# A fused attention and soft mixture-of-experts kernel: blocks 0 and 1 taken in turn by quarters of w_in's columns, raw words and results in one 64 KB tile

## The chip, the core and the metric

The kernel runs on one core of one Trainium2 chip. The metric is the device time of one execution in microseconds (us), lower is better. Engines are named as in the profile: PE is TensorE (matrix products), DVE is VectorE, ACT is ScalarE, POOL is GpSimd, and SP is the queue that issues the DMAs.

## The reference, cut to what matters

Three layers follow one another. The middle one gets its weights `w_in` (512 x 2048) and `w_out` (2048 x 512) as float64 words, which the kernel turns into float32 itself.

```
a  = softmax(x @ state.T / 8);  xread = a @ state
a2 = softmax(state @ x.T / 8);  sread = a2 @ x
y  = concat(xread, sread)                  # 8 batches x 544 rows x 512
h  = y @ w_in;  g = h * sigmoid(h);  z = g @ w_out
logits = z @ phi                           # 32 slots
d = softmax(logits over rows);  c = softmax(logits over slots)
slots = d.T @ z;  out = c @ (relu(slots @ w1[e]) @ w2[e])
```

## The kernel before, in words

**Blocks and steps.** The 8 batches are blocks 0 to 7 of 512 rows each; a ninth, shorter block (number 8) holds the rows of `sread`. For a block k, `a_scores` multiplies its tokens `xT` with the state (PE, tiles `sc`), `a_split`, `a_soft1`, `a_soft2` and `a_soft3` make the softmax on ACT and DVE (tiles `e`, `s`, `asm`, `tm`) and leave it as `ar` in two parts, a rounded one (ACT) and the remainder (DVE for blocks 0 and 1, POOL later). `a_eT` and `a_sread` make `sread` (tiles `eT`, `sr`, `srT`; they need the tokens `xk`). `wb` multiplies the state with a quarter of `w_in`'s columns (tiles `wbp`, `wb`), so that `hid` needs only `ar` and `wb`: its 16 steps j are the heavy part, six PE matmuls of 128x128 by 128x512 each into `h` (the second of the six is the first that needs the remainder of `ar`). ACT or DVE turn `h` into `g`, of which there are six buffers; DVE transposes `g` into the block's store `blk`, and `logits` multiplies it with `w2p` (tiles `lg`). When a block's 16 steps are done, `s_rep` makes its softmax weights (`d`, `dT`, `lT`) and `s_dTg` sums `dT` times `blk` (tiles `S`) into `acc`. After block 8 comes the expert part: its weights w1 and w2, 32 loads of 1 MiB, go into places that earlier tiles have left (`load_w`, lines 1120 to 1155), four of them in the store of block 7 and four in that of block 8.

**The weights.** `w_in` and `w_outT` come as 16 halves of 1 MiB in the order of the list `RAW` (line 29). A half is converted by `conv` (line 634): ACT makes the high part into the result, ACT or DVE (list `LOW_DVE`) makes the low part into the tile `part`, DVE shifts the result and POOL adds `part`. `wo_half` (line 671) also makes `w2p` for a quarter: two PE steps, `w2ps` and `w2q`, with an ACT copy `w2s` between. The 16 halves go through eight slots in two `blk` buffers (line 618).

**The order.** Nothing is issued as written. The `Recorder` (line 183) keeps every operation with a priority: its place in the program, plus shifts, plus a number of the table `RANK` (line 55). `schedule` (line 366) then picks, engine by engine, the operation to go next; `change` (line 397) is what it counts for a change of the PE's tile shape. Every engine and the DMA queue execute their lists strictly in that order. Where the plan has PE waiting in the first 60 us, `filler` puts matmuls of the constant tile `thb` (128x256) there, which write a bank not yet in use.

**Around the change.** Lines 1219 to 1251 start the program: the loads, block 0's softmax, the first scores of block 1. Lines 1255 to 1323 are the main loop over the blocks k and their 16 steps j. Block 0 needs all four quarters of `w_in` before block 1 begins:

```
for k in range(NB):
    for j in range(16):
        hid(k, j)
        ...
        if k == 0 and i == 0 and fq < 3:
            for kind, f in RAW[2 * fq + 2:2 * fq + 4]:
                for half in range(2):
                    (win_half if kind == "win" else wo_half)(f, half)
```

## Time and profile before

| | before |
|---|---|
| median of 3 runs | 454.51 us (453.86 to 455.41) |
| span of the profiled execution | 452.2 us |
| PE busy | 427.8 us (95%) |
| DVE busy | 306.0 us (68%) |
| ACT busy | 276.5 us (61%) |
| POOL busy | 130.3 us (29%) |
| DMA | 92.20 MB, mean 204 GB/s |

The span runs from the first to the last instruction of one profiled execution. That execution is none of the three timed ones, and its own time is known by its span alone, which is 2.3 us under their median. Starts in the rows count from the span's start. PE's busy time includes the filler matmuls, and matmuls of one row overlap those of the next by a little, so that durations on PE are best read from one start to the next.

### The profile page before, as it was taken

How to read it: one execution, taken by the hardware profiler on the slowest of the kernel's cores; microseconds unless marked ns; L12 is line 12 of the kernel's file. 1: busy time of each engine (PE TensorE's matmuls, PEld its weight loads, DVE VectorE, ACT ScalarE, POOL GpSimd, SP SyncE). 2: the span in 40 equal slices, each digit the busy share in tenths (PEclk: the TensorE clock that was granted, in tenths of full speed). 3: DMA queues.
4: the chain of work that ended last, by engine and by line, in shares of the span. 5: the costliest groups of instructions: out<-in, count | busy, mean ns of one | idle time of the engine just before them, and what ended most of it. 6: DMA issues, size and time to landing. Idle time of an engine off the chain costs nothing.

```text
span 452.2 us, 11973 instructions
## 1 busy us (share of the span) xinstructions
PE 427.8 (95%) x5186; PEld 274.6 (61%) x5186; DVE 306.0 (68%) x539; ACT 276.5 (61%) x490; POOL 130.3 (29%) x72
## 2 busy tenths in 40 slices
PE   7889999999999999999999999999999999799980
PEld 6655667658656765775765676487487785334430
DVE  1979878877787787788868779878953405312370
ACT  4899985855767595496768659567568422110270
POOL 1557653232233134124223313321155430000000
PEclk9999999999999999999999999999999999999996
DMA  8999930221402602232060242212293899999998
GB/s 322 424 425 427 392 121 1 96 96 46 187 10 88 233 1 96 86 148 60 39 233 3 94 155 81 94 48 96 79 386 130 328 396 425 398 423 425 403 370 291
DMA packets 22245, 92.20 MB, mean 204 GB/s; under 512 B 1712, under 2 KB 9776, under 8 KB 13744
## 3 DMA queue, kind: packets, MB, share of 16 engines
q1 hardware_dynamic: 22192, 91.43, 52.2%
q8 instruction: 41, 0.67, 0.6%
q14 instruction: 12, 0.10, 0.1%
HBM read 79.37 MB, written 12.06 MB: 202 GB/s over the span
## 4 chain that ended last, share of the span: by engine, by line
PE 80%; DMA 12%; DVE 2%; ACT 2%; issue 1%; SPq 0%; DVEq 0%
PE h L515 45%; PE lg L515 8%; PE S L515 8%; DMA blk<-in_w_dram 7%; PE wbp L515 7%; DMA raw<-in_w_in_dram 4%; DMA xT<-in_xT_dram 2%; PE sc L515 2%; PE sr L515 2%; PE eT L515 1%; PE o L515 1%; PE dT L515 1%; PE gt L515 1%; PE sib L515 1%; DVE place L515 1%; PE f L515 1%
## 5 line engine op out<-in xcount | busy, mean ns | idle before, releaser
L515 PE MATMUL h<-ar,wb 128*128 128x512 f32 x768 | 191.8, 401 | 0.4 <-DVE ar L515 0.4
L515 PEld LDWEIGHTS h<-ar,wb 128*128 128x128 f32 x768 | 139.3, 188 | 46.3 <-issue 12.7
L515 DVE STREAM_TRANSPOSE blk<-g 128x512 f32<-128x512 f32 x128 | 89.0, 702 | 21.5 <-ACT g L515 20.9
L515 ACT ACTIVATE g<-h 128x512 f32<-128x512 f32 x100 | 59.7, 603 | 52.7 <-PE h L515 36.4
L515 POOL TENSOR_TENSOR wb<-wf,wb 128x512 fp32r<-128x512 f32 x26 | 34.6, 1329 | 138.1 <-ACT wf L515 107.9
L515 PEld LDWEIGHTS lg<-g,w2p 128*32 128x32 f32 x1152 | 29.5, 109 | 27.3 <-issue 14.8
L515 PE MATMUL lg<-g,w2p 128*32 128x128 f32 x1152 | 40.3, 275 | 0.3 <-ACT w2p L515 0.3
L515 PE MATMUL S<-blk,dT 32*32 32x512 f32 (+1 forms) x1040 | 38.5, 599 | 0.4 <-ACT dT L515 0.4
L515 ACT CAST wb<-wbp 128x512 fp32r<-128x512 f32 x64 | 34.8, 599 | 4.8 <-PE wbp L515 4.8
L515 PE MATMUL wbp<-win,ss 64*32 64x512 f32 x512 | 33.3, 597 | 1.1 <-POOL win L515 1.1
L515 POOL TENSOR_TENSOR s<-s,tm 128x1024 f32<-128x1024 f32 x12 | 23.2, 1938 | 33.5 <-ACT thb L515 12.7
L515 ACT ACT_TABLE_LOAD x21 | 26.9, 1283 | 6.2 <-DMA raw<-in_w_in_dram 5.8
L515 DVE TENSOR_TENSOR wb<-wbp,wb 128x512 fp32r<-128x512 f32 x38 | 25.6, 679 | 4.6 <-ACT wb L515 4.6
L515 POOL TENSOR_TENSOR acc<-acc,part 128x1024 uint32<-128x1024 uint32 x8 | 19.9, 2489 | 16.3 <-DVE acc L515 10.3
L515 POOL TENSOR_TENSOR win<-win,part 128x1024 uint32<-128x1024 uint32 x8 | 19.0, 2387 | 16.5 <-DVE win L515 11.9
L515 POOL TENSOR_TENSOR wlo<-win,whi 128x1024 fp32r<-128x1024 f32 x8 | 19.0, 2394 | 15.1 <-ACT whi L515 15.1
L515 DVE SCALAR_TENSOR_TENSOR acc<-acc,m,S 128x512 f32<-128x512 f32 x28 | 19.2, 742 | 6.0 <-PE S L515 6.0
L515 DVE SCALAR_TENSOR_TENSOR g<-thb,h 128x512 f32<-128x512 f32 x28 | 18.5, 678 | 6.9 <-ACT thb L515 6.8
L515 PE MATMUL lg<-thb 128*128 128x256 f32 x76 | 20.4, 426 | 1.2 <-DVE thb L515 1.2
L515 PE MATMUL h<-whi,rd 128*128 128x512 f32 x64 | 20.5, 401 | 0.0
L515 DVE TENSOR_REDUCE tm<-s 128x32 f32<-128x1024 f32 x16 | 19.2, 1198 | 0.8 <-ACT s L515 0.8
L515 PEld LDWEIGHTS lg<-thb 128*128 128x128 f32 x76 | 15.9, 217 | 5.3 <-issue 1.7
(158 smaller groups left out, 579.7 us busy)
## 6 DMA issues: line engine op xcount, KB each, us to landing
place<-in_w_dram SPq DMA_DIRECT2D x17, 1024.0 KB, 10.5
blk<-in_w_dram SPq DMA_DIRECT2D x13, 1024.0 KB, 10.1
raw<-in_w_in_dram SPq DMA_DIRECT2D x8, 1024.0 KB, 11.3
xT<-in_xT_dram SPq DMA_DIRECT2D x8, 1024.0 KB, 6.2
raw<-in_w_outT_dram SPq DMA_DIRECT2D x8, 1024.0 KB, 9.6
xk<-in_xk_dram SPq DMA_DIRECT2D x8, 1024.0 KB, 5.7
blk<-in_w_out_dram SPq DMA_DIRECT2D x6, 1024.0 KB, 4.8
out_dram<-place SPq DMA_DIRECT2D x10, 512.0 KB, 6.9
```

What stands on the lines that cost most here:

```text
L515: made = [call(*args, **kwargs) for call, args, kwargs in op.calls]
```

## The change

Blocks 0 and 1 are no longer done one after the other. The list `UNITS_OF` goes through (block, quarter) pairs: quarter 0 of block 0, quarter 0 of block 1, quarter 1 of both, quarters 2 and 3 of block 0, then those of block 1; from block 2 on the order is as before. Block 1's softmax therefore stands ahead of the loop. Conversions come at fixed steps (`CONV_AT`). The stores of even and odd blocks and the raw words are now parts of one tile `big`; a half stays in the slot that `RAW_SLOT` names, its low part is rounded where it stands, and `part` goes. Block 1's four steps by way of the tanh move from quarters 0 and 1 to quarters 2 and 3 (`WINS`). The program text loads block 0's tokens first. The planner's costs for a change of tile shape are new (`CH`), and the table `RANK` is a different, longer one (681 lines in place of 90).

```diff
-RAW = [("win", 0), ("win", 1), ("wo", 0), ("win", 2), ("wo", 1), ("win", 3), ("wo", 2), ("wo", 3)]
+RAW = [("win", 0), ("wo", 0), ("win", 1), ("wo", 1), ("win", 2), ("win", 3), ("wo", 2), ("wo", 3)]
+RAW_SLOT = (0, 4, 1, 5, 2, 3, 6, 7, 2, 3, 6, 7, 3, 6, 7, 6)
+UNITS_OF = [(0, 0), (1, 0), (0, 1), (1, 1), (0, 2), (0, 3), (1, 2), (1, 3)]
+UNITS_OF += [(k, fq) for k in range(2, 8) for fq in range(4)]
+WINS = {0: (0, 0), 1: (9, 13), 8: (0, 2)}
+CONV_AT = {0: 2, 3: 2, 6: 2, 9: 2, 12: 2, 15: 2}
...
 RANK = {
...
-                return 0.1 if mode == FULL or op.mode == FULL else 0.05
-            return 0.55 if mode == (32, 32) and run and len(op.calls) > 8 else 0.0
+                small = (32, 32) in (mode, op.mode)
+                return CH[2 * small + (mode != FULL and op.mode != FULL)]
+            return CH[4] if mode == (32, 32) and run and len(op.calls) > 8 else 0.0
...
+CH = (0.1, 0.09, 0.17, 0.15, 0.55)
...
-    raws = [unit("blk", [4, 1024, 2], f"raw{i}", U32) for i in range(2)]
+    big = one.tile([128, 2, 16 * 512], F32, tag="big", name="big")
...
-            nc.vector.tensor_scalar(out=r, in0=lo, scalar1=2.0**-29, scalar2=2.0**23, op0=ALU.mult, op1=ALU.add)
+            nc.vector.tensor_scalar(out=lo, in0=lo, scalar1=2.0**-29, scalar2=2.0**23, op0=ALU.mult, op1=ALU.add)
         else:
-            nc.scalar.activation(out=r, in_=lo, func=AF.Identity, scale=2.0**-29, bias=ulps)
+            nc.scalar.activation(out=lo, in_=lo, func=AF.Identity, scale=2.0**-29, bias=ulps)
         nc.vector.tensor_scalar(out=d, in0=d, scalar1=3, scalar2=None, op0=ALU.logical_shift_left)
-        nc.gpsimd.tensor_tensor(out=d, in0=d, in1=r, op=ALU.add)
+        nc.gpsimd.tensor_tensor(out=d, in0=d, in1=lo, op=ALU.add)
...
-        bufs[f"b{k}"] = t = unit("blk", [16 * 512], f"blk{k}")
+        bufs[f"b{k}"] = t = big[:, k % 2]
...
+    load_xT(0)
+    nc.sync.dma_start(out=st_sb[:, 0:1], in_=stT[:, 0:1])
     next_raw()
-    nc.sync.dma_start(out=st_sb[:, 0:1], in_=stT[:, 0:1])
-    load_xT(0)
     next_raw()
...
     a_scores(1)
     a_split(1)
     load_xT(2)
+    a_soft1(1)
+    wo_half(0, 0)
+    wo_half(0, 1)
+    a_soft2(1)
+    a_soft3(1)
...
-    for k in range(NB):
+    for p, (k, fq) in enumerate(UNITS_OF):
...
-        for j in range(16):
-            fq, i = divmod(j, 4)
+        for i in range(4):
+            j, t = 4 * fq + i, 4 * p + i
             s = 16 * k + j
             hid(k, j)
...
```

**The start of the DMA queue SP** (`raw` and `big` from `in_w_in` or `in_w_outT` are halves of the weights, `ss` the state, `cst` and `phi` constants). Before:

```order
L515 DMA raw_76<-in_w_in_dram 128x2048 x2
L515 DMA ss<-in_stT_dram 128x128
L515 DMA xT_86<-in_xT_dram 128x2048
L515 DMA raw_76<-in_w_in_dram 128x2048
L515 DMA raw_77<-in_w_in_dram 128x2048
L515 DMA phi<-in_phi_dram 128x128
```

Of the change, from the second row of its list on (the first is two halves from `in_w_outT`):

```order
L1109 DMA ss<-in_stT_dram 128x128
L1109 DMA big<-in_w_in_dram 128x2048
L1109 DMA cst<-in_consts_dram 128x258
L1109 DMA xT_84<-in_xT_dram 128x2048
L1109 DMA big<-in_w_in_dram 128x2048
L1109 DMA xk_85<-in_xk_dram 128x2048
L1109 DMA phi<-in_phi_dram 128x128
L1109 DMA big<-in_w_outT_dram 128x2048
L1109 DMA ss<-in_stT_dram 128x896
L1109 DMA big<-in_w_in_dram 128x2048 x2
L1109 DMA big<-in_w_outT_dram 128x2048
L1109 DMA xT_92<-in_xT_dram 128x2048
```

In the list that results, block 0's tokens (`xT_84`) have three halves ahead of them where there were two, and block 1's (`xT_92`) come after eight halves.

**PE around its first steps of `hid`** (`h_0`, `h_1`; `sc` and `wbp` just ahead of them are block 1's scores and the product for its quarter 0; `lg` from `thb` are fillers). Before:

```order
L515 MATMUL srT_103<-cst,srs_102 128x128
L515 MATMUL lg_134<-thb 128x256 x3
L515 MATMUL h_0_112<-ar_97,wb_94 128x512 x6
L515 MATMUL h_1_118<-ar_97,wb_94 128x512 x6
L515 MATMUL sc_0_105<-xT_98,ss 32x512 x4
L515 MATMUL sc_1_106<-xT_98,ss 32x512 x4
L515 MATMUL wbp_0_0_121<-win_79,ss 32x512 x4
L515 MATMUL wbp_0_1_122<-win_79,ss 32x512 x4
L515 MATMUL w2ps_115<-acc,phi 32x512 x4
L515 MATMUL h_2_123<-ar_97,wb_94 128x512 x6
```

Of the change, first up to block 0's `h_1`, then a piece that ends with block 1's `h_0` and `h_1` (`ar_113` is block 1's `ar`):

```order
L1109 MATMUL w2ps_110<-acc,phi 32x512 x4
L1109 MATMUL lg_150<-thb 128x256 x2
L1109 MATMUL sc_0_103<-xT_92,ss 32x512 x4
L1109 MATMUL sc_1_104<-xT_92,ss 32x512 x4
L1109 MATMUL wbp_0_0_125<-win_77,ss 32x512 x4
L1109 MATMUL wbp_0_1_126<-win_77,ss 32x512 x4
L1109 MATMUL w2q_112<-cst,w2s_111 128x32 x4
L1109 MATMUL h_0_120<-ar_96,wb_93 128x512 x6
L1109 MATMUL h_1_122<-ar_96,wb_93 128x512 x6
```

```order
L1109 MATMUL wbp_0_0_140<-win_78,ss 32x512 x4
L1109 MATMUL wbp_0_1_141<-win_78,ss 32x512 x4
L1109 MATMUL w2ps_131<-acc,phi 32x512 x4
L1109 MATMUL lg_138<-g_1_123,w2p 32x128 x4
L1109 MATMUL lg_138<-g_2_128,w2p 32x128 x4
L1109 MATMUL lg_138<-g_3_130,w2p 32x128 x4
L1109 MATMUL wbp_0_0_152<-win_78,ss 32x512 x4
L1109 MATMUL wbp_0_1_153<-win_78,ss 32x512 x4
L1109 MATMUL w2q_133<-cst,w2s_132 128x32 x4
L1109 MATMUL h_0_134<-ar_113,wb_124 128x512 x6
L1109 MATMUL h_1_136<-ar_113,wb_124 128x512 x6
```

Block 1's scores, its `wbp` and the first `w2q` have gone ahead of the first `h_0`, and block 1's `h_0` comes after only four steps of block 0; before, it came after all 16. Before the first `h` of block 1, PE's list now holds 46 fillers; all of the list before held 42.

**PE in a middle block, around the sums `S`** (block 5's steps, block 4's sums). Before:

```order
L515 MATMUL S_1_1_442<-blk_312,dT_416 32x512 x4
L515 MATMUL lg_432<-g_4_429,w2p 32x128 x4
L515 MATMUL S_0_0_439<-blk_312,dT_416 32x512 x4
L515 MATMUL S_0_1_440<-blk_312,dT_416 32x512 x4
L515 MATMUL S_1_0_441<-blk_312,dT_416 32x512 x4
L515 MATMUL S_1_1_442<-blk_312,dT_416 32x512 x4
L515 MATMUL lg_432<-g_5_431,w2p 32x128 x4
L515 MATMUL lg_432<-g_6_438,w2p 32x128 x4
```

Of the change:

```order
L1109 MATMUL S_1_1_435<-big,dT_409 32x512 x4
L1109 MATMUL lg_425<-g_0_403,w2p 32x128 x4
L1109 MATMUL lg_425<-g_1_405,w2p 32x128 x4
L1109 MATMUL lg_425<-g_2_418,w2p 32x128 x4
L1109 MATMUL S_0_0_432<-big,dT_409 32x512 x4
L1109 MATMUL S_0_1_433<-big,dT_409 32x512 x4
L1109 MATMUL S_1_0_434<-big,dT_409 32x512 x4
L1109 MATMUL S_1_1_435<-big,dT_409 32x512 x4
L1109 MATMUL eT_0_436<-cst,e_393 128x128 x4
L1109 MATMUL h_6_430<-ar_368,wb_413 128x512 x6
```

The four parts of `S` were each followed by a piece of `lg` or by `h`; now three of them stand together and one piece of `lg` is between. Counted over that block, PE's list has 18 stretches of one tile shape where it had 25; over blocks 0 and 1 together it has 47 where it had 54.

## Rows read from the trace of the kernel before

**Rows 1.** The stretches view, TensorE granted clock in `PEclk`; busy microseconds of each engine.

```profile
core 0: us, PE busy (x) PEld busy (x) DVE busy (x) ACT busy (x) POOL busy (x), PEclk, DMA share, GB/s
0.00:30.78 30.78, 24.71 (x182) 18.37 (x182) 19.32 (x29) 22.09 (x27) 12.14 (x9) 1.00 0.95 387
30.78:57.00 26.22, 25.37 (x195) 15.81 (x195) 22.66 (x32) 25.83 (x38) 17.34 (x7) 1.00 1.00 412
134.13:172.69 38.56, 38.56 (x512) 25.24 (x511) 31.16 (x54) 26.34 (x50) 11.48 (x7) 1.00 0.27 97
353.00:397.00 44.00, 40.91 (x437) 26.95 (x435) 15.82 (x47) 12.11 (x22) 6.20 (x3) 1.00 0.98 395
```

**Rows 2.** The chain of waits, first 60 us: start, duration, what.

```profile
2.13 9.27 DMA xT<-in_xT_dram
```

**Rows 3.** The token tile's DMAs, first 60 us; the second of them as SP issued it.

```profile
DMA to landing us min/median/max: 9.3/11.4/16.5
16.71 0.36 SPq L515 DMA_DIRECT2D xT<-in_xT_dram  x1
```

**Rows 4.** PE's groups: out<-in, shape xcount | busy us, mean ns | idle before.

```profile
L515 PE MATMUL lg<-thb 128*128 128x256 f32 x76 | 20.4, 426 | 1.2 <-DVE thb L515 1.2
L515 PE MATMUL wbp<-thb 128*128 128x256 f32 x8 | 2.2, 402 | 0.0
L515 PE MATMUL h<-ar,wb 128*128 128x512 f32 x768 | 191.8, 401 | 0.4 <-DVE ar L515 0.4
L515 PE MATMUL wbp<-win,ss 64*32 64x512 f32 x512 | 33.3, 597 | 1.1 <-POOL win L515 1.1
L515 PE MATMUL sc<-xT,ss 64*32 64x512 f32 x128 | 8.7, 599 | 1.7 <-DMA xT<-in_xT_dram 1.7
L515 PE MATMUL w2ps<-acc,phi 128*32 128x512 f32 x32 | 4.2, 598 | 0.0
L515 PE MATMUL eT<-cst,e 128*128 128x128 f32 x64 | 9.7, 274 | 0.4 <-ACT e L515 0.4
L515 PE MATMUL sr<-xk,e 128*32 128x64 f32 x512 | 8.8, 220 | 0.5 <-ACT e L515 0.5
```

**Rows 5.** TensorE in order of time, early: start, duration, what.

```profile
28.51 0.30 PE L515 MATMUL srT<-cst,srs 128*128 128x128 f32 x1 [0.69 <-DVE srs L515]
```

**Rows 6.** ScalarE in order of time, 36 to 42 us.

```profile
36.62 1.19 ACT L515 ACTIVATE acc<-raw 128x1024 f32<-128x1024 f32 x1
37.68 1.26 ACT L515 ACTIVATE part<-raw,ulps 128x1024 uint32<-128x1024 uint32 x1
38.81 0.60 ACT L515 ACTIVATE g<-h 128x512 f32<-128x512 f32 x1
...
40.40 1.28 ACT L515 ACT_TABLE_LOAD   x1
```

**Rows 7.** GpSimd and VectorE in order of time, early.

```profile
10.18 2.37 POOL L515 TENSOR_TENSOR win<-win,part 128x1024 uint32<-128x1024 uint32 x1 [9.74 <-DVE win L515]
10.45 2.66 DVE L515 TENSOR_SCALAR win<-win 128x1024 uint32<-128x1024 uint32 x1 [0.34 <-ACT win L515]
```

**Rows 8.** TensorE in order of time, a middle block.

```profile
205.97 1.10 PE L515 MATMUL lg<-g,w2p 128*32 128x128 f32 x32
206.99 1.14 PE L515 MATMUL S<-blk,dT 32*32 32x512 f32 x32
208.06 0.44 PE L515 MATMUL lg<-g,w2p 128*32 128x128 f32 x8
208.44 1.14 PE L515 MATMUL S<-blk,dT 32*32 32x512 f32 x32
```

**Rows 9.** TensorE in order of time, the end of block 7.

```profile
348.61 4.46 PE L515 MATMUL S<-blk,dT 32*32 32x512 f32 x128
```

**Rows 10.** The queue SP and the chain of waits near the end.

```profile
353.13 2.05 SPq L515 DMA_DIRECT2D blk<-in_w_dram  x4
407.58 20.30 DMA blk<-in_w_dram
```

More of the change, by code (lines that the diff above doesn't have):

```diff
@@ new lines @@
+    ("7", "ACT", "copy", "ls", 0): 8,
+    ("7", "ACT", "copy", "wb", 0): 548,
+    ("7", "ACT", "copy", "wb", 1): -661,
+    ("7", "ACT", "copy", "wb", 2): -252,
+    ("7", "ACT", "copy", "wb", 4): 110,
+    ("7", "ACT", "copy", "wb", 5): -478,
+    ("7", "ACT", "copy", "wf", 0): -4,
+    ("7", "ACT", "copy", "wf", 1): -32,
+    ("7", "ACT", "copy", "whi", 0): 283,
+    ("7", "ACT", "copy", "whi", 1): -1157,
+    ("7", "ACT", "copy", "whi", 3): -48,
+    ("7", "DVE", "reciprocal", "cm", 0): -15,
@@ new lines @@
+    ("7", "PE", "matmul", "lg", 15): 357,
+    ("7", "PE", "matmul", "wbp", 0): -791,
+    ("7", "PE", "matmul", "wbp", 1): 597,
+    ("7", "PE", "matmul", "wbp", 2): 10,
+    ("7", "PE", "transpose", "dT", 0): -323,
+    ("7", "PE", "transpose", "lT", 0): 46,
+    ("7", "POOL", "tensor_tensor", "wb", 0): 383,
+    ("7", "POOL", "tensor_tensor", "wb", 1): -222,
+    ("7", "POOL", "tensor_tensor", "wlo", 0): -275,
+    ("7", "POOL", "tensor_tensor", "wlo", 1): 18,
+    ("7", "POOL", "tensor_tensor", "wlo", 2): 827,
@@ new lines @@
+    ("8", "ACT", "copy", "thb", 1): 296,
+    ("8", "ACT", "copy", "whi", 0): 140,
+    ("8", "ACT", "copy", "whi", 1): 715,
+    ("8", "ACT", "copy", "whi", 2): 249,
+    ("8", "ACT", "copy", "whi", 3): 637,
+    ("8", "DVE", "memset", "sums", 0): -313,
+    ("8", "DVE", "reciprocal", "cm", 0): 113,
+    ("8", "DVE", "reduce_sum", "cm", 0): 1220,
+    ("8", "DVE", "reduce_sum", "cm", 1): -564,
+    ("8", "DVE", "scalar_tensor_tensor", "acc", 2): -90,
+    ("8", "DVE", "scalar_tensor_tensor", "acc", 3): 180,
@@ new lines @@
+    ("8", "DVE", "tensor_copy", "place", 22): 225,
+    ("8", "DVE", "tensor_copy", "place", 23): 581,
+    ("8", "DVE", "tensor_copy", "siT", 0): -46,
+    ("8", "DVE", "tensor_copy", "thb", 0): 743,
+    ("8", "DVE", "tensor_reduce", "cm", 1): 140,
+    ("8", "DVE", "tensor_reduce", "fin", 0): -127,
+    ("8", "DVE", "tensor_scalar", "cm", 1): 203,
+    ("8", "DVE", "tensor_scalar", "fin", 0): 871,
+    ("8", "DVE", "tensor_scalar", "fin", 1): -10,
+    ("8", "DVE", "tensor_scalar", "sums", 0): -20,
@@ new lines @@
+    ("8", "DVE", "tensor_tensor", "cw", 0): 62,
+    ("8", "DVE", "tensor_tensor", "cw", 1): 529,
+    ("8", "DVE", "tensor_tensor", "cw", 3): -45,
+    ("8", "DVE", "tensor_tensor", "fin", 0): 90,
+    ("8", "DVE", "tensor_tensor", "fin", 2): 801,
+    ("8", "DVE", "tensor_tensor", "fin", 3): 477,
+    ("8", "DVE", "transpose", "place", 0): 921,
+    ("8", "DVE", "transpose", "sibTs", 1): -104,
+    ("8", "PE", "matmul", "S", 3): -201,
+    ("8", "PE", "matmul", "S", 4): -1185,
+    ("8", "PE", "matmul", "S", 5): 491,
@@ new lines @@
+    ("m", "PE", "matmul", "lg", 3): -394,
+    ("m", "PE", "matmul", "lg", 4): 21,
+    ("m", "PE", "matmul", "lg", 6): -78,
+    ("m", "PE", "matmul", "lg", 7): 728,
+    ("m", "PE", "matmul", "lg", 8): 104,
+    ("m", "PE", "matmul", "lg", 9): 4,
+    ("m", "PE", "matmul", "lg", 10): -331,
+    ("m", "PE", "matmul", "lg", 11): -132,
+    ("m", "PE", "matmul", "lg", 13): 33,
+    ("m", "PE", "matmul", "lg", 15): 203,
+    ("m", "PE", "matmul", "sc", 0): 697,
+    ("m", "PE", "matmul", "wbp", 0): -683,
@@ L145 @@
+    ("m", "PE", "matmul", "wbp", 2): -112,
+    ("m", "PE", "matmul", "wbp", 3): 384,
+    ("m", "PE", "transpose", "eT", 0): -314,
+    ("m", "PE", "transpose", "lT", 0): -318,
+    ("m", "PE", "transpose", "srT", 0): 130,
+    ("m", "POOL", "tensor_tensor", "s", 0): 19,
+    ("m", "POOL", "tensor_tensor", "wb", 1): -516,
+    ("m", "SP", "dma_start", "xT", 0): 32,
+    ("m", "SP", "dma_start", "xk", 0): 362,
 }
@@ L873, in hid @@
         n = ntok(k)
-        if j == 0 and k:
+        if j == 0 and k > 1:
             nc.block(k)
@@ L1228, in tile_state_attention_soft_moe @@
     next_raw()
+    next_raw()
     load_xk(0)
     nc.sync.dma_start(out=st_sb[:, 1:], in_=stT[:, 1:])
-    for _ in range(5):
+    for _ in range(4):
         next_raw()
```

815 lines of the change are left out of this document (666 added, 149 removed).

## The prediction

> **What bounds the kernel now.** I read the stretches first. From 57 us on PE is busy without a gap in every middle block (38.56 us, all of it busy) while DVE and ACT have room; only the first 57 us are different [rows 1]. There PE is busy too, but partly with fillers, so the stretches must be read with the groups of PE: fillers take 20.4 and 2.2 us [rows 4], and PE stands idle for 30.78 - 24.71 = 6.1 us up to the first `h` that has all of block 0's `ar`, and for another 26.22 - 25.37 = 0.9 us up to 57 us [rows 1]. So **29.5 us of the start are not work**. In those stretches the DMA queues are full (0.95 and 1.00) and ACT is nearly so: 25.83 of 26.22 us [rows 1]. The granted clock is 1.00 in each of these stretches, the full 2.4 GHz, so the clock has no part in this.
>
> Near the end the bound changes. When the sums of block 7 are done (they start at 348.61 and take 4.46 us, [rows 9]), their store is free and SP issues four expert loads at 353.13 [rows 10]. From there on the DMA share is 0.98 and the last load, issued at 407.58, needs 20.30 us to land [rows 10], because it stands behind the others; the output follows. So up to block 7's sums a microsecond of PE is a microsecond of the whole, and whatever moves these sums moves the loads and the end with them.
>
> The sum is made against the span, 452.2 us; the median of the runs is 2.3 us above it, and I add the sum to the median. Up to 1.36 us (0.3%) about what a measurement can tell from no change.
>
> **The start: when work is there.** Block 0's tokens landed at 2.13 + 9.27 = 11.40 us [rows 2], as the third MiB. Block 1's were issued at 16.71 [rows 3]; of the three landing times, 16.5 is the one that fits their place as MiB 11.69, so they landed at 33.2. That is (33.2 - 11.4) / (11.69 - 3.06) = 2.53 us a MiB. In the list that the planner has now made, the tokens are not first: block 0's come as MiB 4.19, so they land at 14.3, 2.9 us later. Block 1's are still MiB 11.69: 33.2 us.
>
> Block 0's softmax chain moves by those 2.9 us: its last PE step `srT`, at 28.51 before [rows 5], comes at 31.4. The first `h` then does not start, though: in PE's list `w2ps`, block 1's scores, `wbp` and `w2q` stand ahead of it. The scores wait for the tokens, 33.3, and end at 34.3; `h_0` follows at about 36.7. This alone costs little, since those steps had to be done anyway.
>
> What costs is the next thing. Block 1's `h_0` now comes after four steps of block 0, so block 1's softmax, which had until 74 us before, becomes a chain that PE waits for. I follow it through ACT's list. After `w2ps` at 32.5 ACT converts two more halves and copies `w2s` (2 x 1.06 + 0.5 us), so the copies of the new scores start at 35.8 with PE's end at 34.3 no longer the bound. From these copies to the cast of block 1's `ar` the list holds, start to next start [rows 6]: four conversions (2 x 1.06, from 36.62 to 37.68; 2 x 1.13, from 37.68 to 38.81), one table load (1.28), eleven half-size copies or evictions at the 0.5 us that follow 38.81, four full-size exponentials or casts (about 1.0 each) and one small one: 4.4 + 1.3 + 5.4 + 4.0 = **15 us**. I add 1.7 us of waiting for DVE (a maximum and a subtraction have to come between) and 2.2 us for DVE's remainder of `ar` with what stands ahead of it. 35.8 + 15 + 1.7 + 2.2 = 54.7, so I take **55 us** for the second matmul of block 1's `h_0`.
>
> The work PE has in its list up to there, from the groups [rows 4] by 16, 8, 6, 4 or 64 matmuls a step: four `h` (1.5 each), four `wbp` (1.04), two `sc` (1.09), two `w2ps` and two `w2q` (1.05), four `eT` (0.61), two `sr` (1.1), two `srT` (0.3) and four `lg` (0.3): 22.7 us, less 0.1 for the overlap at each of some 22 borders, 20.5 us. So 55 - 20.5 = 34.5 us of the start are not work, against 29.5: **+5.0 us**. From below, PE does without the waits for this chain and loses only what the fillers say, 46 in its list against 42: 4 x (20.4 + 2.2) / 42 = +2.2 us. From above, the chain is held up by POOL twice over (below): +9.7 us.
>
> **What is taken away.** Two table loads of ACT go, as both softmaxes now come before the first eviction; this is in the 15 us. Rounding in place takes no instruction away: ten halves by ACT and six by DVE as before. The strided result has no row, the strided source has: 1.13 us a half on ACT [rows 6]; I cost it at nothing, covered by DVE's room, and if it is slower the start only gets worse. The tile `part` frees room that nothing uses.
>
> **The middle blocks.** Here each change of tile shape shows. A piece of four `lg` between two parts of `S` takes 206.99 - 205.97 = 1.02 us, a piece of one 208.44 - 208.06 = 0.38 [rows 8]: 0.21 a step and 0.16 for the detour. The sums in a row cost nothing extra: 4.46 / 4 = 1.12 [rows 9] against 1.14 for one that stands alone [rows 8]. The list has two such detours fewer in a block, another piece of `lg` is merged, and `h` stands in five stretches instead of eight: seven changes fewer, 0.3 us for the detours and some 0.1 for the rest, **-0.4 us** in each of blocks 2 to 7, -2.4 together (bounds -1.2 and -3.1, without the rest and with all seven at 0.16 / 2). Blocks 0 and 1 have seven changes fewer too: -0.3. PE must not run dry for this, and the six buffers of `g` are the tight place: eight steps of `h` now stand in a row.
>
> **The end.** In the list before, the sums of block 7 had three matmuls of block 8's third `h` ahead of them, and now they have none: 3 x 0.25 [rows 4] = -0.7 us. The loads behind them are the same 28, so the rest moves as a whole.
>
> Sum: +5.0 - 0.3 - 2.4 - 0.7 = +1.6 us. **454.5 + 1.6 = 456.1 us.**
>
> **Rivals.** *The start is not that late.* If ACT and DVE bring block 1's `ar` by the time PE has worked off its list, the start costs +2.2: 2.2 - 3.4 = -1.2, 453.3 us. It ends on the other side, not slower, and decides where the second matmul of block 1's `h_0` starts before 53 us. For it: two table loads fewer on an ACT that is full. Against it: 15 us of ACT in a row after 35.8. Chance 0.35; a better start or a full 3.1 us from the middle puts most of it under 453.15.
>
> *POOL in the way.* A small scalar operation of DVE stands in block 1's chain while POOL has two additions of a weight half in a row. At 10.45 a shift of DVE, 0.68 us elsewhere, took 2.66 us, until POOL's 2.37 us addition was over [rows 7]. If one such wait falls into the chain, +2.4: 458.5 us. Chance 0.2. The Trainium skill states this as a rule (SBUF — State Buffer, Who interferes with whom): the port that both share is taken for a whole instruction, by whichever starts first. The rows agree, 2.66 us; by that rule the sum would be the 458.5 us of this rival.
>
> *The middle gives nothing.* Eviction after a run of eight `h` leaves PE waiting as long as it saves: 1.6 + 2.4 = +4.0, 458.5 us. Chance 0.15; against it, ACT has 12 and DVE 7 us of room in a block [rows 1].
>
> *The change does not do what it says.* Blocks in turn and the shared tile are in the lists; tokens first is not, and is not counted.
>
> **The numbers.** Forecast 0.3 (it lies 0.2 us above the bound of slower, so its chance is split, 0.18 slower and 0.12 the same). The first rival gives faster 0.23 and the same 0.12, the two others slower. Faster 0.24, the same 0.26, slower 0.50 with the rounding. The range reaches to both sides' cases: 453.3 less the rest of the middle's bound, 451.5, and the 458.5 of two rivals plus part of the upper bound of the start, 460. The forecast's own range is 454.5 to 458.
>
> **What would show it.** Right: block 0's tokens land at about 14, its first `h` starts at 36 to 37, the second matmul of block 1's first `h` at 54 to 56; a middle block takes 38.1 to 38.2 us; block 7's sums end at 354 to 355; from there 99 us to the end, as before. Wrong: if middle blocks take under 37.9, or PE's lost time in the start is under 30 us, or the end after the sums is shorter than 98 us, it is faster than I say.

## The result, and the profile after

The changed kernel takes **460.31 us** (median of 4 runs, 459.7 to 461.7) where the kernel before takes 454.25 us in the same comparison (4 runs, 453.86 to 455.41): a ratio of 1.012, 95% interval 1.0103 to 1.0137. The prediction was 456.1 us, range 451.5 to 460.0. It had the sign; the size was too small by 4.2 us, and the result lies 0.3 us outside the range. One execution of `after_eT` (2355 us) and one of `hyb_end` (461.6 us) count as slow and are not in their ratios.

| | before | after |
|---|---|---|
| median | 454.25 us | 460.31 us |
| span of the profiled execution | 452.2 us | 457.8 us |
| mean granted clock of PE | 0.991 | 0.982 |
| PE busy | 427.8 us (95%) | 431.6 us (94%) |
| ACT busy | 276.5 us (61%) | 272.4 us (60%) |

The span grew by 5.6 us. It is read first in stretches of the changed kernel (busy us of each engine, granted clock, DMA share, GB/s): the start, two pieces of it, one middle block, the stretch between the sums of blocks 6 and 7, and the rest.

```profile
core 0: us, PE busy (x) PEld busy (x) DVE busy (x) ACT busy (x) POOL busy (x), PEclk, DMA share, GB/s
0.00:55.86 55.86, 47.56 (x423) 32.30 (x423) 42.33 (x59) 40.65 (x54) 21.86 (x13) 0.94 0.89 353
14.20:16.00 1.80, 1.75 (x17) 0.52 (x18) 1.80 (x1) 0.19 (x1) 1.36 (x1) 0.67 1.01 428
43.00:46.00 3.00, 3.00 (x63) 2.31 (x66) 2.47 (x6) 2.83 (x4) 0.45 (x1) 0.58 0.70 276
131.67:170.18 38.51, 38.50 (x511) 25.98 (x510) 33.52 (x58) 27.14 (x51) 12.99 (x8) 1.00 0.33 111
323.20:353.19 29.99, 29.99 (x362) 21.11 (x362) 17.71 (x31) 17.52 (x31) 10.85 (x6) 1.00 0.55 211
353.19:457.80 104.61, 86.72 (x1063) 47.43 (x1062) 37.00 (x89) 29.16 (x65) 9.49 (x4) 0.95 0.97 377
```

PE in order of time in the start, with the fillers of the first 60 us as one group behind it:

```profile
14.25 1.51 PE L1109 MATMUL sc<-xT,ss 64*32 64x512 f32 x16 [2.95 <-DMA xT<-in_xT_dram]
...
28.43 1.10 PE L1109 MATMUL sr<-xk,e 128*32 128x64 f32 x64 [0.71 <-ACT e L1109]
...
33.99 1.09 PE L1109 MATMUL sc<-xT,ss 64*32 64x512 f32 x16 [0.34 <-DMA xT<-in_xT_dram]
...
36.78 2.98 PE L1109 MATMUL h<-ar,wb 128*128 128x512 f32 x12
41.65 0.72 PE L1109 MATMUL eT<-cst,e 128*128 128x128 f32 x4 [1.89 <-ACT e L1109]
...
44.94 1.35 PE L1109 MATMUL sr<-xk,e 128*32 128x64 f32 x64
...
55.86 6.41 PE L1109 MATMUL h<-ar,wb 128*128 128x512 f32 x27
```

```profile
L1109 PE MATMUL lg<-thb 128*128 128x256 f32 x92 | 25.7, 433 | 1.2 <-DVE ulps L1109 1.2
```

The start looks as forecast: block 0's scores begin at 14.25, its first `h` at 36.78, block 1's first `h` at 55.86. Of these 55.86 us, 55.86 - 47.56 = 8.3 are idle and 25.7 are fillers: 34.0 us are not work, against 29.5 before. Behind the gaps of 2.95 and 1.89 us the granted clock is 0.67 and 0.58 in the mean, so in part the lower of its two levels (1.2 and 2.4 GHz), and the steps there take longer: `sc` 1.51 us at 14.25 and 1.09 at 33.99, `sr` 1.35 us at 44.94 and 1.10 at 28.43. In the profiled execution of the kernel before it was 1.00 in these stretches [rows 1].

The gap of 1.89 us is PE's wait for ACT's exponentials `e`. VectorE, GpSimd and ScalarE in order of time show what stands behind it:

```profile
35.85 4.80 POOL L1109 TENSOR_TENSOR acc<-acc,big 128x1024 uint32<-128x1024 uint32 x2 [3.06 <-DVE acc L1109]
...
38.28 2.40 DVE L1109 TENSOR_SCALAR asm<-asm 128x2 f32<-128x2 f32 x1
...
40.78 0.72 ACT L1109 ACTIVATE e<-e,asm 128x512 f32<-128x512 f32 x1 [3.24 <-DVE asm L1109]
...
44.05 0.15 DVE L1109 TENSOR_SCALAR asm<-asm 128x2 f32<-128x2 f32 x1
```

DVE's two-number operation on block 1's maxima takes 2.40 us, to the end of POOL's second addition (35.85 + 4.80 = 40.65); its twin at 44.05 takes 0.15. A shift of DVE had met the same before [rows 7]. ACT stands idle for 3.24 us over it. This is the forecast's second rival, POOL in the way, at the place that it named. The Trainium skill (SBUF — State Buffer, Who interferes with whom) says of POOL and a DVE instruction in a two-port mode, which it says `tensor_scalar` can enter, that whoever issues first gets the shared pair of ports for its whole instruction; these rows agree, 2.40 us against 0.15.

Where the 5.6 us lie is read from the first sums of each block. Block 1's sums start at 131.67 (before: 127.79), block 5's at 285.46 (281.99), block 6's at 323.20 (317.83), block 7's at 353.19 (348.61 [rows 9]). So +3.9 us up to block 1's sums, +4.6 up to block 7's, and another +1.0 behind them: 104.61 us against 103.59. The lateness at block 1's sums understates the start: in the changed order the middle sums stand ahead of six matmuls of `h` and a set of four `eT` that were done before them in the old order. They are worth 2.1 us by their busy times and 1.8 from start to next start (six `h` 1.47, a set of `eT` 0.35 in the kernel before). That comes due between the sums of blocks 5 and 6 (`h` x97 instead of x91, `eT` x8 instead of x4). So the start with blocks 0 and 1 really costs 5.7 to 6.0 us, and what lies between gives back 1.1 to 1.4.

At the end SP issues the four expert loads at 357.71, 4.58 us later than before [rows 10], and the last of the loads at 413.65, 6.07 us later; the output follows that.

```profile
357.71 2.11 SPq L1109 DMA_DIRECT2D big<-in_w_dram  x4
...
413.65 0.33 SPq L1109 DMA_DIRECT2D place<-in_w_dram  x1
```

### The profile page after: what moved, and what is told of

The parts are those of the page before. It is cut to its first block, busy times and chain, and to the rows that moved or that the text cites. A ratio compares the mean times of both kernels' runs of the same rounds, so it can differ in the third digit from the quotient of the medians.

```text
span 457.8 us, 12011 instructions
## 1 busy us (share of the span) xinstructions
PE 431.6 (94%) x5194; PEld 282.1 (62%) x5194; DVE 311.2 (68%) x539; ACT 272.4 (60%) x488; POOL 131.9 (29%) x72
## 4 chain that ended last, share of the span: by engine, by line
PE 79%; DMA 13%; DVE 3%; ACT 1%; issue 1%; SPq 1%; DVEq 0%; ACTq 0%
PE h L1109 44%; PE lg L1109 8%; PE S L1109 8%; DMA place<-in_w_dram 7%; PE wbp L1109 6%; DMA big<-in_w_in_dram 6%; PE eT L1109 2%; PE o L1109 2%; PE sr L1109 2%; PE sc L1109 1%; PE so L1109 1%; PE dT L1109 1%; DVE place L1109 1%; PE w2ps L1109 1%; PE sib L1109 1%; DVE asm L1109 1%
## 5 line engine op out<-in xcount | busy, mean ns | idle before, releaser
L1109 PE MATMUL h<-ar,wb 128*128 128x512 f32 x768 | 187.0, 396 | 0.0
L1109 DVE STREAM_TRANSPOSE big<-g 128x512 f32<-128x512 f32 x128 | 86.6, 696 | 23.6 <-ACT g L1109 19.5
L1109 POOL TENSOR_TENSOR wb<-wf,wb 128x512 fp32r<-128x512 f32 x26 | 35.1, 1350 | 105.6 <-ACT wb L1109 82.1
L1109 PE MATMUL S<-big,dT 32*32 32x512 f32 (+1 forms) x1040 | 38.5, 598 | 0.4 <-ACT dT L1109 0.4
L1109 PE MATMUL lg<-g,w2p 128*32 128x128 f32 x1152 | 38.1, 275 | 0.0
L1109 POOL TENSOR_TENSOR win<-win,big 128x1024 uint32<-128x1024 uint32 x8 | 20.2, 2525 | 24.2 <-DVE win L1109 19.5
L1109 PE MATMUL lg<-thb 128*128 128x256 f32 x92 | 25.7, 433 | 1.2 <-DVE ulps L1109 1.2
L1109 POOL TENSOR_TENSOR acc<-acc,big 128x1024 uint32<-128x1024 uint32 x8 | 19.4, 2427 | 24.4 <-DVE acc L1109 23.8
L1109 PEld LDWEIGHTS lg<-thb 128*128 128x128 f32 x92 | 19.3, 219 | 6.1 <-issue 2.1
L1109 PEld LDWEIGHTS S<-big,dT 32*32 32x32 f32 (+1 forms) x1040 | 13.9, 103 | 13.9 <-issue 8.9
L1109 POOL TENSOR_TENSOR ar<-s,ar 128x1024 fp32r<-128x1024 f32 x6 | 14.6, 2436 | 25.8 <-ACT ar L1109 25.8
```

The costliest lines, as they stand in the source:

```text
L1109: made = [call(*args, **kwargs) for call, args, kwargs in op.calls]
```

## The experiments

In all of them the metric is that of the result, and each ratio is against the kernel before on the same chip. A kernel whose *lists are held* gets the order of every engine from a table of indices instead of the planner:

```
+ORDER = [ ... ]
...
-            pick = min(cands, key=lambda c: (c[1].prio, c[0], c[1].idx))
+            op = self.ops[next(todo)]
```

**The tile and the rounding in place, alone** (`tile_only`: the planner orders again, by the old table).

```
-    raws = [unit("blk", [4, 1024, 2], f"raw{i}", U32) for i in range(2)]
+    big = one.tile([128, 2, 16 * 512], F32, tag="big", name="big")
-            nc.scalar.activation(out=r, in_=lo, func=AF.Identity, scale=2.0**-29, bias=ulps)
+            nc.scalar.activation(out=lo, in_=lo, func=AF.Identity, scale=2.0**-29, bias=ulps)
```

> The kernel before with the shared 64 KB tile and the rounding in place, nothing else: blocks in order, the table of before. Theory A (the loss is made in the first 56 us, by the turns of blocks 0 and 1): within 1 us of the kernel before, ratio 0.998 to 1.002, block 7's sums start at 348 to 349.5. Theory B (the new order from block 2 on and at the end makes it): the same. Theory C (the rounding in place, with a strided result, and the later release of raw words make it): 2 us or more above the kernel before, with fillers and idle time of PE in the start over 31 us.

466.63 us, ratio 1.0267 (1.0239 to 1.0295). By its letter theory C came true: far over 2 us, and 7.5 us idle and 25.7 us of fillers in the first 57 us, 33.2 together. But that is only 3.7 us more than before, and block 1's sums are 11.7 us late (139.52). PE in order of time shows the largest other part: between 77 and 104 us PE, which had no gap there before, is idle for 5.2 us, waiting on the second weight's conversion and on evictions.

```profile
90.06 1.08 PE L515 MATMUL w2q<-cst,w2s 128*128 128x32 f32 x8 [1.15 <-ACT w2s L515]
...
98.02 3.01 PE L515 MATMUL h<-ar,wb 128*128 128x512 f32 x12 [1.47 <-DVE g L515]
```

**The same with every list held** to that of the kernel before (`pin_tile`).

> The shared tile and the rounding in place alone, as in tile_only, but with every engine's list held to that of the kernel before, instruction by instruction, fillers too. If the tile itself costs time (raw words live until POOL's addition, so the loads behind them start later), 3 us or more above the kernel before, with SP's loads of raw words late after 26 us. If tile_only's 12 us came from the lists that the planner made from the old table, 454 to 456 us.

455.07 us, ratio 1.0013 (0.9990 to 1.0036): no difference that can be measured. So tile_only's 12 us are not the tile's, and theory C's 2 us or more are not there; they are the lists that the planner makes when the old table of ranks meets slightly other dependencies. The table fits one program. The raw words do live longer. SP's waits from 14 to 60 us, in the kernel before and then in `pin_tile`, show by whom a slot is given free:

```profile
SPq L515 <- DVE part L515: 16.4, 4, 6.1
SPq L515 <- ACT part L515: 8.0, 4, 4.8
```

```profile
SPq L495 <- POOL acc L495: 15.9, 3, 7.8
SPq L495 <- POOL win L495: 12.8, 4, 5.6
```

Before, a load waited for the two reads of ACT and DVE; now it waits for POOL's addition. That this costs time is not shown. Block 1's sums start 1.8 us later here (129.59), but in `hyb_end` below, with the same tile and the same lists up to there, they start where they did in the kernel before (127.79):

```profile
127.64 1.14 PE L495 MATMUL S<-big,dT 32*32 32x512 f32 x32
```

The two executions part early. Ahead of block 0's scores PE was idle for 2.21 us in `pin_tile` and for 1.73 in `hyb_end`, and from 14 to 16 us the granted clock was 0.53 in the one and 1.00 in the other.

**The tables** (`in_order_new_tables`: tile_only with the new ranks and switch costs from block 2 on; `after_old78` and `after_oldm78`: the changed kernel with the old ranks for block 7 and the end, and for blocks 2 to 6 as well).

```
 RANK = {
-    ("7", ...): <changed kernel>, ("8", ...): <changed kernel>
+    ("7", ...): <kernel before>, ("8", ...): <kernel before>
```

> As tile_only, and with the changed kernel's table and switch costs for the middle blocks, block 7 and the end: what is left out of the change is the turns of blocks 0 and 1 and their table. Theory A: 453.5 to 455 us, since only the start costs; a middle block of 38.4 us. Theory B: about 456 us, 1.8 us above the kernel before (0.7 up to the sums of block 7 and 1.1 behind them, as the two traces show them).

> The changed kernel with the old table for block 7 and the end. Theory A: 460.3 us, within 0.7. Theory B: 458.0 to 459.2 us: the 1.1 us behind block 7's sums goes, and perhaps some of the 1.9 us that the stretch from block 5's to block 6's sums got longer.

> The changed kernel with the old table for blocks 2 to 7 and the end; only the start and its table are the changed ones. Theory A: 460 to 461.5 us, a middle block of 38.5 us, the lost time of the start (fillers and idle PE up to 55.9 us) still 34 us. Theory B: 458.5 us (1.8 us less).

470.35 us (1.034, 1.0319 to 1.0361), 461.33 us (1.0138, 1.0117 to 1.0158) and 470.16 us (1.0335, 1.0300 to 1.0370). Of these times only after_old78's can be read: other ranks at the end change nothing. The two others again measure a table on a program that it was not made for; from here on I held the lists.

The trace of `after_old78` shows more than its time. Up to block 7 its engines' lists are those of the changed kernel, yet DVE's operation on the maxima did not wait in the profiled execution:

```profile
38.36 0.12 DVE L826 TENSOR_SCALAR asm<-asm 128x2 f32<-128x2 f32 x1
```

```profile
112.39 1.14 PE L826 MATMUL S<-big,dT 32*32 32x512 f32 x32
```

Block 1's first `h` starts at 53.66 there, 2.20 us earlier than in the changed kernel; block 0's sums come 2.23 us earlier (112.39 against 114.62), block 1's 2.23 (129.44) and block 5's still 2.08 (283.38). So the wait comes and goes between executions of the same lists. Only one of the changed kernel's four timed executions was profiled, and it had the wait; for the others that is not known.

**The start and the rest apart** (`hyb_bstart`, `hyb_astart`: held lists, the one order up to block 1's first sum and the other behind it; both with the shared tile).

```
-ORDER = [ all of one kernel ]
+ORDER = [ one kernel's up to the first sum of block 1 ] + [ what remains, in the other's order ]
```

> Shared tile and rounding in place; every engine's list is that of the kernel before up to the first sum of block 1, and from there on the instructions that remain, in the changed kernel's order (no turns, but the new order of the middle blocks, of block 7 and of the end). If only the start costs: 454 to 455.5 us, sums of block 7 at 347 to 349. If the new order from block 2 on costs too: 456 us or more (1 us and more lost between block 1's sums and the end).

> The changed kernel's lists up to the first sum of block 1 (the turns, its loads, its fillers), and from there on the kernel before's order. If only the start costs: 459.5 to 462 us. If the new order from block 2 on costs 1.5 us: 458 to 459 us.

hyb_bstart takes 456.57 us, ratio 1.0051 (1.0035 to 1.0068), with block 7's sums at 350.69. Compared with the changed kernel's 460.31, the changed start costs 3.7 us, against an old start that was 1.8 us late at block 1's sums in this trace too (129.63). Compared with pin_tile's 455.07, the new order behind block 1 costs about 1.5 us, 1.12 of which is one wait at the seam:

```profile
139.09 1.09 PE L495 MATMUL wbp<-win,ss 64*32 64x512 f32 x16 [1.12 <-DVE acc L495]
```

hyb_astart takes 466.44 us (1.0272, 1.0251 to 1.0293) and tells little: the old order behind a start with turns makes PE wait 1.91 and 3.19 us at the seam. From block 1's first sum to the end it needs 324.3 us, like the kernel before (324.4); the changed kernel needs 326.1, with the 1.8 us of put-off work among it.

**Tokens really first** (`pin_tokens`: lists held, only SP's order changed).

```
-SP: big, big, ss, big, cst, xT, big, xk, ...
+SP: xT, ss, big, big, big, cst, big, xk, ...
```

> The changed kernel with every list held but SP's: block 0's tokens and its state are loaded first, ahead of the first raw words, as the order in which the code is written has it. If the lateness of block 0's tokens costs time, about 3 us less than the changed kernel (457.5). If the start is bound by block 1's chain or by the raw words, 460 us within 1, or up to 2.5 us more, since two halves of raw words land later.

463.32 us, 1.0190 (1.0167 to 1.0213): 3.0 us more than the changed kernel, and already 3.0 at block 0's sums (117.61 against 114.62). So the raw words rather than block 0's tokens lead the start; a MiB put ahead of them costs about what it takes to land (2.5 us by the forecast's reading).

**The fillers** (`pin_nofill` without them, `more_fill` with eight more, lists held).

```
 ORDER, where -n stands for n fillers (two matmuls each):
-changed kernel:  ... -19 ... -13 ... -2 -3 -2 -2 -1 -1 -3 ...
+pin_nofill:      ... no negative number ...
+more_fill:       ... -24 ... -13 ... -2 -3 -2 -2 -3 -1 -1 -3 ...
```

> The changed kernel with all lists held and the 92 fillers of PE taken out (they compute nothing that is used). If the fillers only stand in waiting time, their 25.7 us turn into idle time and the end moves by under 1 us, or later by 1 to 3 us where the granted clock falls without them. If they delay the work behind them, the end comes 2 us or more earlier.

> The changed kernel with all lists held and eight more fillers: five ahead of block 0's scores and three ahead of block 1's first transposes, where PE stood idle for 2.95 and 1.89 us and the granted clock fell to 0.67 and 0.58 behind them. If the low clock behind these gaps costs, 0.5 to 1.5 us less than the changed kernel, and the clock stays at 1.00 from 14 to 20 and from 40 to 46 us. If it doesn't, the same within 0.3%, or later by what the fillers overrun.

Without fillers 462.69 us, 1.0186 (1.0156 to 1.0217), 2.4 us more than with them: they stand in waiting time, and without them the early steps take nearly twice as long:

```profile
14.31 1.96 PE L503 MATMUL sc<-xT,ss 64*32 64x512 f32 x16 [14.31 <-DMA xT<-in_xT_dram]
```

The same step takes 1.09 us elsewhere. The profile's clock column reads 1.00 in this stretch all the same, so the durations decide here.

With eight more fillers 460.81 us, 1.0144 (1.0127 to 1.0162), the same. The clock stays at 1.00 and block 1's first `h` starts 1.6 us earlier, as the clock's theory had it; 13 us later PE waits 1.05 us for an eviction of ACT, so that block 0's sums are only 0.35 us earlier.

```profile
14.20:16.00 1.80, 1.80 (x20) 0.88 (x17) 1.80 (x2) 0.73 (x2) 1.14 (x1) 1.00 1.01 428
43.00:46.00 3.00, 2.59 (x70) 2.00 (x70) 2.69 (x6) 2.97 (x5) 1.82 (x1) 1.00 0.73 262
```

```profile
54.25 11.17 PE L503 MATMUL h<-ar,wb 128*128 128x512 f32 x48
...
68.94 0.43 PE L503 MATMUL lg<-g,w2p 128*32 128x128 f32 x8 [1.05 <-ACT g L503]
```

But the clock is not shown by this. The eight fillers move the work by half a microsecond, and the small operation of DVE now slips in between POOL's two additions (35.37 + 4.83 / 2 = 37.79):

```profile
35.37 4.83 POOL L503 TENSOR_TENSOR acc<-acc,big 128x1024 uint32<-128x1024 uint32 x2 [3.06 <-DVE acc L503]
...
37.79 0.13 DVE L503 TENSOR_SCALAR asm<-asm 128x2 f32<-128x2 f32 x1
```

So two things changed at once. `hyb_astart`, whose start has the changed kernel's lists, parts them by chance: the operation waited there as well, and the clock stayed at 1.00.

```profile
38.15 2.38 DVE L503 TENSOR_SCALAR asm<-asm 128x2 f32<-128x2 f32 x1
```

```profile
43.00:46.00 3.00, 2.56 (x73) 2.01 (x73) 2.79 (x7) 2.98 (x4) 0.60 (x1) 1.00 0.82 341
```

Its block 1's first `h` starts at 55.36, 0.5 us before the changed kernel's and 1.7 behind after_old78's: most of the delay is the wait, not the clock.

**The port alone** (`free_port`: the changed kernel with lists held; fillers as they are, one shift of DVE behind the small operation, so that POOL's second addition starts later).

```
-DVE: shift acc, big, shift acc, s, asm max, s, asm, tm max, ...
+DVE: big, shift acc, s, asm max, s, asm, shift acc, tm max, ...
```

> The changed kernel with its lists held and one instruction moved: VectorE's shift of one half of w_out (the source of the second of GpSimd's two additions in a row) stands behind the small scalar operation on block 1's maxima. In the changed kernel that operation took 2.40 us, from 38.28 until GpSimd's second addition ended at 40.65, where it takes 0.13 to 0.17 us elsewhere; ScalarE waited 3.24 us for it and TensorE then 1.89 us for the exponentials. The port theory (the rival 'POOL in the way' came true): the operation takes under 0.3 us, ScalarE's exponentials start some 2 us earlier, block 1's first h starts at 53.5 to 54.5 instead of 55.86, and the clock between 43 and 46 us stays at 1.00, without a filler more. Of the end: if that wait decides the time, 458.0 to 458.6 us (ratio 1.008 to 1.0095); if the conversions of the raw words are a second bound just beneath it, 459.8 to 460.7 (1.0115 to 1.0140) and block 0's sums at most 0.5 us earlier than 114.62. If the clock and not the port was what the eight further fillers mended, block 1's first h stays at 55.5 to 56.

The mechanism came as the port theory said. In DVE, ACT and PE in order of time and in the windows:

```profile
38.65 0.12 DVE L505 TENSOR_SCALAR asm<-asm 128x2 f32<-128x2 f32 x1
...
38.86 0.72 ACT L505 ACTIVATE e<-e,asm 128x512 f32<-128x512 f32 x1 [0.97 <-DVE asm L505]
...
54.13 11.32 PE L505 MATMUL h<-ar,wb 128*128 128x512 f32 x48
```

```profile
14.20:16.00 1.80, 1.67 (x16) 0.26 (x16) 1.80 (x1) 0.00 (x0) 1.34 (x1) 0.52 1.00 423
43.00:46.00 3.00, 2.25 (x62) 1.65 (x50) 2.80 (x7) 2.97 (x4) 1.63 (x1) 1.00 0.88 341
```

The operation takes 0.12 us, block 1's first `h` starts at 54.13, 1.73 us earlier, and the clock from 43 to 46 us is 1.00 with no filler more (behind the gap at 14, which is still there, it is 0.52). So in the changed kernel the fall of the clock there came with the wait and not the other way round; hyb_astart shows that the wait need not bring it. Block 0's sums start at 113.51, 1.11 us earlier, block 7's at 352.12, 1.07 earlier: more than the second bound's 0.5, less than the whole 1.73, and half of what after_old78 shows. Here POOL's second addition ends 1.2 us later than in the changed kernel (41.87 against 40.65), which after_old78 does not have; that this takes the difference is not shown. Three traces with the wait and the same lists have block 0's sums at 114.14 (hyb_astart), 114.62 and 115.11 (after_eT), so a single pair of traces is good to about half a microsecond. The time is 459.52 us against 455.2 in this comparison (medians 1.0095 apart; ratio 1.012, 1.0086 to 1.0154, its six runs from 458.9 to 463.9). That can't be told from the changed kernel's. The span is 457.5 us, only 0.3 shorter, for behind block 7's sums 105.4 us follow instead of 104.6. The queue SP shows where the 1.07 us go:

```profile
394.76 8.13 SPq L505 DMA_DIRECT2D place<-in_w_dram  x5
...
408.50 0.33 SPq L505 DMA_DIRECT2D place<-in_w_dram  x1
```

The group of five is issued 1.08 us earlier than in the changed kernel (395.84), the load that waits for its landing 0.13 earlier (408.63): in the chain of waits the transfer between takes 12.86 us instead of 11.92. From 395 to 425 us the DMA share is 1.01 in both kernels. With the queue full, being early earns little. Five traces with the changed kernel's end say the same: with block 7's sums at 351.83 (no_chain1, below), 352.12, 352.89 (more_fill), 353.19 (the changed kernel) and 353.82 us (after_eT, below) the span ends at 458.0, 457.5, 458.0, 457.8 and 458.0.

**Block 1's chain** (`no_chain1`, `no_chain1_loads`).

```
-    a_scores(1)
-    a_split(1)
...
-    a_sread(1)
+    at[1, "ar"] = at[0, "ar"]
```

> The changed kernel with all lists held and block 1's scores, softmax and state read left out (30 instructions; block 1 takes block 0's results instead, its loads stay), with the fillers that stood ahead of them. If PE waits for that chain, 8 us or more less than the changed kernel (452 or below): 3.7 us of PE's own work and the 4 to 6 us of idle time and fillers between 39.7 and 48 us. If the raw words and their conversion are the bound there, only the work goes or less: 456.5 to 460 us.

> As no_chain1 (block 1's scores, softmax and state read left out, block 0's results taken), and block 1's two MiB of tokens are not loaded either. If the queue of loads is the second bound of the start (raw words that wait behind tokens), the 3 us waits of ACT for raw words between 38 and 54 us shrink and the end comes 3 us or more earlier than no_chain1: 457 us or less. If slots of the shared tile bound the raw words, no change against no_chain1 within 1.5 us.

460.48 us, 1.0104 (1.0062 to 1.0145; its six runs from 455.5 to 461.8), and 457.89 us, 1.0077 (1.0059 to 1.0095). Leaving out the chain, and with it the wait at the port, four fillers and 3.7 us of PE's own work, brings block 1's sums 1.38 us earlier (130.29), hardly more than free_port and less than after_old78, and no change of the time can be told. ACT's rows tell why it isn't more: in the start it now stands waiting for raw words for 6.9 us, of which there was 0.19 us in the changed kernel.

```profile
44.69 1.12 ACT L501 ACTIVATE win<-big 128x1024 f32<-128x1024 f32 x1 [1.95 <-DMA big<-in_w_in_dram]
...
53.62 2.22 ACT L501 ACTIVATE win<-big 128x1024 f32<-128x1024 f32 x2 [3.11 <-DMA big<-in_w_in_dram]
```

Two MiB fewer in the queue bring 2.6 us by the medians (460.48 to 457.89), though the intervals overlap, and 1.4 at block 7's sums (351.83 to 350.41); two long waits of ACT stay (2.89 and 2.69 us). So the queue is perhaps part of this second bound. Whether the rest is the slots, which SP's waits above suggest, was not tried.

**The order of the middle and of the end** (`after_eT`, `before_eT`, `hyb_end`).

```
-PE, blocks 2 to 6 after:  S eT h h eT wbp
+PE, after_eT:             S eT h eT h wbp
-PE, blocks 2 to 6 before: h eT h | S h h wbp lg h h eT h
+PE, before_eT:            h h | S eT h h eT wbp lg h h h
```

> The changed kernel with all lists held, but that in blocks 2 to 6 the second transposes eT of a block stand one step of h earlier, between two steps of h instead of ahead of wbp. If a step's price hangs on what stands next to it (eT 0.35 us between two h, 0.53 ahead of wbp, start to next start), the period of a middle block falls by 0.1 to 0.2 us from 38.4 to 38.5. If only the number of changes between 128x128 and smaller tiles counts, it stays within 0.03 us, as their number is the same.

> The kernel before with all lists held, but that in blocks 2 to 6 the two transposes eT stand where the changed kernel has them: the first directly behind the sums, the second ahead of wbp; ACT's copy of the first moves with it. By the changed kernel's rows (0.41 and 0.53 us instead of 0.35 and 0.35, and one stretch of h fewer broken) the period of a middle block rises by 0.1 to 0.25 us over 38.55. If only the number of changes between 128x128 and smaller tiles counts, it stays within 0.03 us or falls.

> Shared tile and rounding in place; the lists of the kernel before up to the first sum of block 6, and the changed kernel's order for what remains (block 7's second half, block 8, the expert loads, the output). The prediction's view, the end moves as a whole with block 7's sums: those sums come 30.0 us after block 6's instead of 30.8, and 103.6 to 104.2 us later the span ends, 0.3 to 1 us less than pin_tile in all. If the new order of the end itself costs: 104.6 us or more behind the sums, 0.3 to 1.5 us more than pin_tile.

after_eT: 460.57 us, 1.0129 (1.0107 to 1.0152), a period of 38.45 to 38.46 us from sums to sums, as in the changed kernel (38.39 to 38.47). What `eT` gains in its new place (0.36 instead of 0.53) the broken stretch of `h` loses. before_eT: 455.91 us, 1.0026 (1.0012 to 1.0041), a period of 38.69 to 38.72 instead of 38.55: +0.16 a block at the same number of changes. Neither view holds for both: the count of changes fails in before_eT, the price by neighbours in after_eT.

hyb_end: 456.44 us, 1.0048 (1.0023 to 1.0072), its runs spread from 454.7 to 461.6. Block 7's sums come 30.88 us after block 6's, not 30.0, and 104.9 us later the span ends. The new end perhaps costs 1 us, but the interval overlaps that of pin_tile, and the stretch behind block 7's sums differs by 0.6 us between two kernels of the same lists (103.6 before, 104.2 in pin_tile).

## Why the prediction was right and wrong

**The start: its signs came by luck, because two errors met.** Tokens at 14, first `h` at 36.8, block 1's first `h` at 55.9, 34.0 us that are not work (34.5 forecast, +4.5 instead of +5.0). With "-0.3" for the shapes of blocks 0 and 1 the forecast was +4.7; measured is 5.7 to 6.0. The wait at the port accounts for 1.1 (free_port) to 2.2 of it (after_old78): without it the start costs 3.5 to 4.9. So ACT's chain was forecast too long (55 us; without the wait block 1's first `h` starts at 53.7 to 54.1), and the rival that it was weighed against came on top. Part of that is a slip: 32.5 and the forecast's own 2 x 1.06 + 0.5 make 35.1, not 35.8, for the first copy of the new scores, and ACT began it at 35.27. PE's work up to there adds up to 23.0, not 22.7. Seen as PE's time, the 1.2 to 1.5 us beyond the 34.0 are work that takes longer: up to block 1's sums PE's time other than fillers and the start's idle time was 98.3 us before and is 97.7 now, though 1.8 to 2.1 us of work were put off. 0.42 us of `sc` and 0.25 of `sr` at the lower clock are among it. The sentence that the clock has no part held for one execution of the kernel before; the last section has the others.

**POOL in the way: it came, at the place named, was given a chance of 0.2, and stood in the sum at nothing.** Its price of 2.4 us was the duration (2.25 us more than the twin). It is worth 2.2 us at the sums where the same lists ran without it, 1.1 where an instruction was moved to avoid it, and there 0.3 us at the end of the span. Whether it happens is a matter of little: the operation began at 38.28, when POOL's first addition (half of 4.80 us from 35.85) had ended at about 38.25. By the same estimate it began 0.03 to 0.05 us behind that end in the four traces with the wait (the changed kernel, after_eT, hyb_astart, pin_tokens), and 0.01 us behind it or before it in the four without that have the two additions in a row (after_old78, after_oldm78, more_fill, pin_nofill). A list that looks the same does not settle it.

**The middle blocks: wrong, and this is the step that failed first.** It said that seven changes of shape fewer give -0.4 us a block. Blocks 2 to 5 have periods of 38.39, 38.47 and 38.42 us against 38.55, which looks like -0.12. But pin_tile, with the old lists instruction for instruction, has 38.44:

```profile
206.51 1.14 PE L495 MATMUL S<-big,dT 32*32 32x512 f32 x32
...
221.39 7.06 PE L495 MATMUL h<-ar,wb 128*128 128x512 f32 x30
...
244.95 1.14 PE L495 MATMUL S<-big,dT 32*32 32x512 f32 x32
```

So the seven changes are worth **nothing**, within 0.05 us. They are not all changes of tile shape, either: three of the seven are borders between `h` and the transposes, whose rows have the same tile (128*128); by the tile there are 16 stretches in a block before and 12 now. The bounds for this term (-1.2 and -3.1) do not follow from its own 0.3 and 7 x 0.08 us in six blocks either, which give -1.8 and -3.4. The reading that misled stands in the rows: the forecast set 4.46 / 4 = 1.12 us for sums in a row [rows 9] against 1.14 for one that stands alone [rows 8] and concluded that a row costs nothing extra. But 1.14 is the busy time, which overlaps the next row; from start to next start one alone takes 208.06 - 206.99 = 1.07 [rows 8]. In the changed kernel three in a row take 3.34, 1.11 each:

```profile
208.57 3.40 PE L1109 MATMUL S<-big,dT 32*32 32x512 f32 x96
211.91 0.86 PE L1109 MATMUL lg<-g,w2p 128*32 128x128 f32 x24
212.70 1.16 PE L1109 MATMUL S<-big,dT 32*32 32x512 f32 x32
213.79 0.66 PE L1109 MATMUL eT<-cst,e 128*128 128x128 f32 x4
214.20 3.02 PE L1109 MATMUL h<-ar,wb 128*128 128x512 f32 x12
217.06 0.60 PE L1109 MATMUL eT<-cst,e 128*128 128x128 f32 x4
217.59 1.95 PE L1109 MATMUL wbp<-win,ss 64*32 64x512 f32 x32
```

The steps from the first sum to the one behind the last take 213.79 - 208.57 = 5.22 us, with 24 `lg` among them. Before they took 6.27, with 56: the 32 further `lg` at 0.031 (64 in 1.99 us) are 1.0, so two detours fewer gave 0.05, where 2 x 0.16 had been put in. And the transposes `eT` take 0.41 and 0.53 us here, from start to next start, where they took 0.35 between two steps of `h`: 0.24 a block is given back there.

**Blocks 6 and 7: -0.7 forecast.** The three matmuls are gone, 29.99 us instead of 30.78. Between the sums of blocks 5 and 7 the changed kernel nevertheless needs 67.73 us instead of 66.62, because the work that had been put off comes due.

**The end: it moved, but not as a whole.** The last load moved by 6.1 us for 4.6 of the sums, and 104.6 us follow where 99 + 4.5 were meant. "The rest moves as a whole" failed: with the sums 1.07 us earlier the span shrank by 0.3, and with sums from 351.83 to 353.82 it hardly moved at all. Where the 1.0 us more come from is not settled.

Together, with the put-off work at 2.1 us: +6.0 where +4.7 was forecast, -1.4 where -3.1 was, +1.0 where 0 was, and 0.2 that the median moved more than the span: 5.8 instead of 1.6 us. Of the error of 4.2 us the gain between blocks 1 and 7 has 1.7, the start 1.3, the end 1.0 (2.0, 1.0 and 1.0 with the put-off work at 1.8). So the steps that failed are the middle's gain, priced by busy times; the wait behind POOL, left out of the sum; and an end that was to move with the sums. Two rivals came out together, POOL in the way and "the middle gives nothing" (though not by its mechanism: PE never waited for evictions there). At the forecast's own prices both make 456.1 + 2.4 + 2.4 = 460.9, 0.6 us from the result. That closeness is partly luck, since the end's 1.0 us belongs to neither and the chain was forecast too long. The text had set the two beside each other at 458.5 each and ended its range at 460; that both could be true had no place in it.

No version beat the kernel before; the nearest, pin_tile and before_eT, equal it or lie 0.3% above it.
